# Two of the four set-aside scores of an attention turn, computed and copied in halves of 256 queries

## The chip, the cores and the metric

The kernel runs on one core of a Trainium2 chip. The metric is the device time of one execution in microseconds (us). A run of the kernel before took 1273.32 us (the median of three, from 1272.75 to 1273.88).

## The reference, cut to what matters

```python
def reference(A_x, A_wqkv, A_wo, B_x, B_w1, B_b1, B_w2, B_b2):
    xn = layernorm(A_x)                                   # (1, 2048, 512)
    qkv = (xn @ A_wqkv).reshape(B, S, 3, 32, 16)          # 32 heads of 16
    scores = einsum("bhqd,bhkd->bhqk", q, k) * 16 ** -0.5
    s = (softmax(scores) @ v) @ A_wo                      # (1, 2048, 512)
    h = relu(xn @ B_w1 + B_b1) ** 2                       # 512 -> 1792
    g = silu(h @ B_w2 + B_b2)                             # 1792 -> 512
    return A_x + s * g
```

All of it is in float32. Attention has 32 heads and 2048 x 2048 scores for each.

## The kernel before, in words

**Stages.** A first stage (about the first 150 us) normalizes x, projects queries, keys and values, and stores queries and keys, each as a high and a low part, so that one contraction over 64 rows gives the score of one head in nearly full precision. Then comes the long stage that the change is in: 128 turns, from about 150 us to about 1250 us. A tail multiplies the last attention output by wo.

**Steps and turns.** A step (`steps`) is one group of four heads (`qd`), one chunk of 512 queries (`qc`) and one block of 128 keys (`kb`): 8 x 4 x 16 = 512 steps. Each step has four heads: pair `p` in 0, 1 and half `hp` in 0, 1. `score(i, p, hp, dst)` is one matmul of 64 rows by 128 columns by 512 queries; `hp` 0 uses the upper 64 rows of the TensorE array and `hp` 1 the lower 64, so two matmuls of different `hp` that follow each other run beside each other. A turn handles four steps. For three of them, `scores(i, p)` computes both heads of a pair into one of two two-bank PSUM tiles (tag S), and `exps(i, p, src)` takes the exponential of both on ScalarE, from PSUM into an SBUF tile `ptile[i, p]`.

**The set-aside step.** The fourth step of a turn, `i + 3`, does not use the S tiles. Its four heads go one at a time through a single PSUM bank, the tile `single` of 128 x 512 float32: `aside(i, p, hp)` issues the score matmul into `single` and a VectorE copy from `single` into half of `ptile[i, p]`. Later ScalarE takes the exponential of `ptile[i, p]` in place. There is one such bank, so each set-aside matmul has to come after the copy of the one before.

**What fills the array.** The feed-forward layer (and later the projection by wo) is spread over the turns as blocks of matmuls of 64 rows by 128 columns by 512. `lin(0)` issues the next one for the upper 64 rows, `lin(1)` for the lower, `lin(0, 1)` one of each; they accumulate in the two banks of the tile `spare`. Next to a set-aside score, which uses only half of the rows, stands a single `lin` of the other half: `lin(0)` with a score of `hp` 1, `lin(1)` with one of `hp` 0.

**Order of a turn.** It is written out by hand. TensorE, VectorE and ScalarE each run their instructions in this order; the framework adds the semaphores. In 120 of the 128 turns the second branch below is taken. (The other branch, which the change leaves alone, belongs to the 8 turns whose block both begins and ends in the same turn.)

```python
        else:
            lin(0)
            aside(i + 3, 0, 1)
            exps(i + 2, 0, scores(i + 2, 0))
            lin(0, 1)
            lin(0, 1)
            exps(i + 2, 1, scores(i + 2, 1))
            aside(i + 3, 1, 0)
            lin(1)
            exps(i + 3, 0, ptile[i + 3, 0])
```

Ahead of it stand the two `scores` of step `i + 1`, with the first set-aside score beside a `lin(1)` between them, and four `lin(0, 1)`; behind it four `lin(0, 1)` and the two `scores` of step `i + 4`, with the fourth set-aside score beside a `lin(0)` ahead of the second of them.

At the end of a turn, `values(i)` to `values(i + 3)` multiply the exponentials of the four steps by the values, into the bank `acc` (line 538). What VectorE has to do besides (evicting `spare`, splitting weights, row sums) is issued at the turns' ends.

**Lines.** In the profile line 282 is the score matmul (its output is named S or `lin`; `lin` is the tag of the tile `single`), line 305 the copy of a set-aside score, line 286 the exponential, line 330 a matmul of the filling work, line 538 the values.

Of the kernel before, what the change touches and what calls it, by code (L numbers as in the profile page):

```python
# [46 lines left out]
@with_exitstack  # L47
def mha_ffn_kernel(ctx: ExitStack, tc: tile.TileContext, x, wqkv, wo, bx, w1, b1, w2, b2, out):
    nc = tc.nc
    x, out = x[0], out[0]  # L50
    ctx.enter_context(tc.manual_schedule())
    keep = ctx.enter_context(tc.tile_pool(name="keep", bufs=1))
    dram = ctx.enter_context(tc.tile_pool(name="dram", bufs=1, space=DRAM))

    ident = keep.tile([128, 128], FT, name="ident")
    make_identity(nc, ident)
    vt = keep.tile([128, NK, VW], FT, name="vt")
    nvalid = keep.tile([1, 1], I32, name="nvalid")
    stat = keep.tile([128, 80], FT, name="stat")

    kdram = [[dram.tile([128, 2, 1024], FT, name=f"kd{g}_{h}") for h in range(2)] for g in range(4)]
    qdram = [[dram.tile([128, 2, 512], FT, name=f"qd{g}_{c}") for c in range(NC)] for g in range(4)]
    xdram = [dram.tile([128, 2, 4, 512], FT, name=f"xd{c}") for c in range(3)]

    udram = [[dram.tile([2, 2, 16, 4, 512], FT, name=f"ud{g}_{c}") for c in range(NC)] for g in range(4)]
    zdram = [[dram.tile([4, 512], FT, name=f"zd{q}_{c}") for c in range(NC)] for q in range(NQ)]
    gdram = dram.tile([S, D], FT, name="gd")

    with tc.tile_pool(name="sb", bufs=1) as sb, tc.tile_pool(name="ps", bufs=1, space=PSUM) as ps:
        fast_path(tc, sb, ps, locals())  # L70
    general_path(tc, dram, nvalid, ident, vt, kdram, qdram, gdram, x, wo, out)


def fast_path(tc, sb, ps, env):
# [6 lines left out]
    mm = nc.tensor.matmul  # L81
    dve, act, pool, sp = nc.vector, nc.scalar, nc.gpsimd, nc.sync
# [3 lines left out]
    def t(shape, dt, tag):  # L86

        cnt[0] += 1
        p = ps if tag in ("S", "lin", "acc") else sb
        if tag in BUFS:  # L90
            turn[tag] = turn.get(tag, -1) + 1
            n = turn[tag] % BUFS[tag]
            tag = f"{tag}{places[n] if tag == 'S' else n}"
        return p.tile(shape, dt, tag=tag, name=f"{tag}_{cnt[0]}")
# [180 lines left out]
    steps = [(qd, qc, kb) for qd in range(NQ) for qc in range(NC) for kb in range(NK)]  # L275
    ptile = {}

    def score(i, p, hp, dst):
        qd, qc, kb = steps[i]
        k, q = ka[qd, kb // 8], qa[qd, qc]  # L280
        r = slice(64 * hp, 64 * hp + 64)
        mm(dst, k[r, p, 128 * (kb % 8):128 * (kb % 8) + 128], q[r, p], start=True, stop=True)  # L282

    def exps(i, p, src):
        if src is not None:
            act.activation(ptile[i, p], src, AF.Exp, scale=SCALE)  # L286

    def place(i, p):
        ptile[i, p] = t([128, 2, 512], FT, f"P{2 * ((i - 1) % 4) + p}")

    def scores(i, p):

        if i < len(steps):
            sc = t([128, 2, 512], FT, "S")
            place(i, p)
            for hp in range(2):
                score(i, p, hp, sc[:, hp])
            return sc

    def aside(i, p, hp):  # L300

        if hp == 0:
            place(i, p)
        score(i, p, hp, single)
        dve.tensor_copy(ptile[i, p][:, hp], single)  # L305

    gated, complete, gates = {}, set(), set()

# [30 lines left out]
    def lin(*halves):  # L339
        if pair[0]:  # L340
            for half in halves:
                j = half ^ swapped[0]
                pair[0][j].issue(half, lin_banks[j])

    def swap():
        if pair[0]:
            while any([pair[0][half ^ swapped[0]].issue(half, lin_banks[half ^ swapped[0]]) for half in range(2)]):
                pass
            swapped[0] ^= 1
            if not swapped[0]:  # L350
                pair[0][0].evict()
                pair[0] = None
# [21 lines left out]
    def split_piece(eng=None):  # L374
        if at_piece[1] == len(pieces):
            return
        j, layer, m = pieces[at_piece[1]]
        at_piece[1] += 1
        raw, q = raws.pop(0), PAIRS[m][1]
        wf[layer, m] = [t([128, 4, 256] if layer == 1 else [128, 2, 512], FR, f"wf{layer}{p}{q}") for p in "hl"]  # L380
        split(*wf[layer, m], raw, eng or dve, pool)
        load_piece()
# [149 lines left out]
    def values(i):  # L532
        qd, qc, kb = steps[i]
        if kb == 0:
            acc[0] = t([128, 512], FT, "acc")
        for j in (1, 2, 3, 0) if i % 2 else (0, 1, 2, 3):
            o = (4 * qd + j) * 17
            mm(acc[0][32 * j:32 * j + 32], vt[:, kb, o:o + 32], ptile[i, j // 2][:, j % 2],  # L538
               start=kb == 0, stop=kb == NK - 1)

    def finish(i):

        qd, qc, kb = steps[i]
        if kb < NK - 1:
            return
        if i == len(steps) - 1:
            return
        ou = t([128, 512], FT, "ou")
        cast(act if turn_ends_first[0] else dve, ou, acc[0])
        sp.dma_start(zdram[qd][qc], ou[16::32])  # L550
        for j in range(4):
            sp.dma_start(udram[qd // 2][qc][0, qd % 2, :, j], ou[32 * j:32 * j + 16])
        n = i // 4
        events.setdefault(2 * n + 2, []).insert(0, (load_sums, (qd, qc)))
        at(n + 2, rowsums, qd, qc)
# [174 lines left out]
    def happen(time):  # L730
        for fn, a in events.pop(int(2 * time), ()):
            fn(*a)


    n = turn["S"]
# [4 lines left out]
    single = t([128, 512], FT, "lin")  # L740
    xs[0] = xT[3]

    def rest(i, dst):

        group(dst, lambda p: onorm[2, 3][p][:, cut[i]], lambda p: wos[0][p][:, 3])

    def end_rest(i, src):

        o = t([128, 512], FT, f"wf2{'hl'[i // 2]}{i % 2}")
        dve.scalar_tensor_tensor(o, src, 0.5, gsb[2, i // 2][:, i % 2], op0=OP.mult, op1=OP.mult)  # L750
        pool.dma_start(out[1024 + 128 * i:1152 + 128 * i], o, accum_op=OP.add)

    turn_ends_first = [False]
    for n in range(TURNS):
        i = 4 * n
        happen(n)
        make, end, split_now = fill[n]
        if make:
            pair[0] = make()
        exps(i + 1, 0, scores(i + 1, 0))  # L760
        aside(i + 3, 0, 0)
        lin(1)
        exps(i + 1, 1, scores(i + 1, 1))
        for _ in range(5 if make and end else 4):
            lin(0, 1)
        if make and end:
# [3 lines that stand above are left out]
            swap()  # L770
# [5 lines that stand above are left out]
            last = [scores(i + 4, 0)]  # L776
            for _ in range(4):
                lin(0, 1)
        else:
            lin(0)  # L780
            aside(i + 3, 0, 1)
            exps(i + 2, 0, scores(i + 2, 0))
            lin(0, 1)
            lin(0, 1)
            exps(i + 2, 1, scores(i + 2, 1))
            aside(i + 3, 1, 0)
            lin(1)
            exps(i + 3, 0, ptile[i + 3, 0])
            lin(0, 1)
            lin(0, 1)  # L790
            last = [scores(i + 4, 0)]
# [3 lines that stand above are left out]
        aside(i + 3, 1, 1)  # L795
        exps(i + 3, 1, ptile[i + 3, 1])
        last.append(scores(i + 4, 1))
        for p in range(2):
            exps(i + 4, p, last[p])
        if n == TURNS - 1:  # L800
            two = t([128, 2, 512], FT, "S")
            rest(0, two[:, 0])
        turn_ends_first[0] = n < LAST and end and fill[n][0] is None and fill[n - 1][2] and n % per in (7, 15, 23)
        swap()
        if n == LAST - 1:
            gsb.update({(2, i): y[2, i] for i in range(2)})
        if n == TURNS - 1:
            end_rest(0, two[:, 0])
        happen(n + 0.5)
        if split_now:  # L810
            split_piece()
        for j in range(4):
            values(i + j)
        finish(i + 3)
# [5 lines left out]
    zc, r = t([128, 16], FT, "zc"), t([128, 16], FT, "rc")  # L820
# [15 lines left out]
    for i in range(4):  # L836
        for j in range(4):
            mm(small[32 * j:32 * j + 32, 0, cut[i]], r[:, 4 * i + j:4 * i + j + 1].broadcast_to([128, 32]), ident,
               start=True, stop=True)
# [138 lines left out]
```

## Time and profile before

| | before |
|---|---|
| median of 3 runs | 1273.32 us |
| profiled execution, its time | 1272.96 us |
| span in the profile | 1271.1 us |
| TensorE matmuls (PE) | 1257.3 us busy, 9925 instructions |
| TensorE weight loads (PEld) | 721.4 us busy |
| ScalarE (ACT) | 1034.2 us busy |
| VectorE (DVE) | 678.5 us busy, 1065 instructions |
| granted TensorE clock | 0.998 |

The span runs from the first to the last instruction that the profiler recorded; the profiled execution's time is 1.86 us longer. PE is the matmul side of TensorE and PEld its weight loads, which have rows of their own. A matmul's recorded duration includes its way through the array, so two that follow each other overlap in the records: how often one can start is read from the start times, not from the durations.

### The profile page before, as it was taken

The page shows a single profiled execution, that of the slowest core. Times are in us where ns is not written, and L with a number is a line of the kernel's source. Part 1 is how long each engine was busy: PE and PEld are TensorE (multiplying, and loading weights), DVE is VectorE, ACT ScalarE, POOL GpSimd, SP SyncE. Part 2 cuts the span into 40 slices and gives each one's busy share as a digit, 9 for nine tenths or more (in the row PEclk, how much of TensorE's full clock was granted, in tenths as well). Part 3 has the DMA queues.
Part 4 walks back from the last instruction along what each step waited for, and adds up shares of the span by engine and source line. Part 5 has one row for each costly group of instructions (what it writes and reads, how often), then busy time and mean ns, then how long its engine had stood idle before and what let it go on. Part 6 is the DMA issues. An engine that isn't in the chain of part 4 may idle for free.

```text
span 1271.1 us, 24788 instructions
## 1 busy us (share of the span) xinstructions
PE 1257.3 (99%) x9925; PEld 721.4 (57%) x9925; DVE 678.5 (53%) x1065; ACT 1034.2 (81%) x1123; POOL 257.8 (20%) x149
## 2 busy tenths in 40 slices
PE   9999999999999999999999999999999999999996
PEld 7888755555555455555555555555555555545553
DVE  5542255455555654545465455555554545566655
ACT  4222588889899898898988889899889988998883
POOL 5000122122211221312022221220331212322111
PEclk9999999999999999999999999999999999999999
DMA  7565513131233132121423222333222132463445
GB/s 266 206 232 197 217 43 102 58 93 59 77 125 109 59 105 64 45 87 48 152 73 109 60 76 60 93 125 108 58 60 87 47 89 59 142 216 125 143 129 118
DMA packets 84940, 137.32 MB, mean 108 GB/s; under 512 B 26058, under 2 KB 40408, under 8 KB 83284
## 3 DMA queue, kind: packets, MB, share of 16 engines
q1 hardware_dynamic: 81668, 126.25, 30.9%
q0 software_dynamic: 2720, 8.65, 2.3%
q8 instruction: 79, 1.29, 0.4%
q10 hardware_dynamic: 432, 0.79, 0.2%
q14 instruction: 41, 0.34, 0.1%
HBM read 94.24 MB, written 41.41 MB: 107 GB/s over the span
## 4 chain that ended last, share of the span: by engine, by line
PE 96%; DVE 2%; ACT 1%; POOL 0%; DMA 0%; issue 0%; ACTq 0%; DVEq 0%
PE acc L538 36%; PE spare L330 26%; PE S L282 16%; PE S L111 9%; PE lin L282 7%; DVE P L305 1%; PE S L204 1%; POOL hl L104 0%; DMA P<-in_A_x_dram 0%; PE acc L111 0%; DVE st L166 0%; DVE P L858 0%; ACT P L286 0%; DVE P L864 0%; ACT wf2h L98 0%
## 5 line engine op out<-in xcount | busy, mean ns | idle before, releaser
L286 ACT ACTIVATE P<-S 128x1024 f32<-128x1024 f32 x768 | 732.4, 1020 | 67.9 <-PE S L282 64.5
L305 DVE COPY P<-lin 128x512 f32<-128x512 f32 x512 | 354.1, 692 | 467.6 <-PE lin L282 342.7
L538 PE MATMUL acc<-P,vt 128*32 128x512 f32 x4096 | 466.0, 595 | 0.0
L282 PE MATMUL S<-QA,KA 64*128 64x512 f32 x1536 | 332.8, 422 | 0.1
L286 ACT ACTIVATE P<-P 128x1024 f32<-128x1024 f32 x256 | 271.4, 1060 | 43.7 <-DVE P L305 43.6
L538 PEld LDWEIGHTS acc<-P,vt 128*32 128x32 f32 x4096 | 120.2, 110 | 272.9 <-issue 272.9
L282 PEld LDWEIGHTS S<-QA,KA 64*128 64x128 f32 x1536 | 145.3, 184 | 159.9 <-ACT P L286 142.6
L282 PE MATMUL lin<-QA,KA 64*128 64x512 f32 x512 | 213.2, 416 | 1.0 <-DVE P L305 0.3
L104 POOL TENSOR_TENSOR wf1l<-wr,wf1h 128x1024 fp32r<-128x1024 f32 x28 | 66.8, 2384 | 404.5 <-DVE wf1h L100 135.3
L330 PE MATMUL spare<-xl,wf1h 64*128 64x512 f32 x504 | 122.3, 400 | 0.0
L104 POOL TENSOR_TENSOR hl<-T,hh 128x1024 fp32r<-128x1024 f32 x28 | 67.6, 2415 | 242.2 <-PE S L282 131.3
L104 POOL TENSOR_TENSOR wf2l<-wr,wf2h 128x1024 fp32r<-128x1024 f32 x28 | 66.7, 2383 | 207.4 <-PE acc L538 139.1
L330 PE MATMUL spare<-wf2l,hh 64*128 64x512 f32 x448 | 107.1, 399 | 0.0
L282 PEld LDWEIGHTS lin<-QA,KA 64*128 64x128 f32 x512 | 94.2, 184 | 22.3 <-DVE P L305 13.6
L330 PE MATMUL spare<-xh,wf1l 64*128 64x512 f32 x504 | 96.3, 392 | 0.0
L330 PE MATMUL spare<-xh,wf1h 64*128 64x512 f32 x504 | 95.5, 390 | 0.0
L330 PE MATMUL spare<-wf2h,hh 64*128 64x512 f32 x448 | 87.7, 392 | 0.0
L330 PE MATMUL spare<-wf2h,hl 64*128 64x512 f32 x448 | 84.6, 391 | 0.0
L330 PEld LDWEIGHTS spare<-xl,wf1h 64*128 64x128 f32 x504 | 67.0, 185 | 8.2
L330 PEld LDWEIGHTS spare<-xh,wf1h 64*128 64x128 f32 x504 | 60.0, 185 | 9.8
L330 PEld LDWEIGHTS spare<-xh,wf1l 64*128 64x128 f32 x504 | 59.8, 185 | 8.4
L98 ACT CAST P<-S 128x512 fp32r<-128x512 f32 x30 | 17.6, 587 | 57.7 <-PE S L111 55.9
(201 smaller groups left out, 995.6 us busy)
## 6 DMA issues: line engine op xcount, KB each, us to landing
wr<-in_B_w_dram SPq DMA_DIRECT2D x56, 512.0 KB
KA<-kd SPq DMA_DIRECT2D x64, 256.0 KB
QA<-qd SPq DMA_DIRECT2D x128, 128.0 KB
kd<-P SPq DMA_DIRECT2D x15, 512.0 KB
qd<-P SPq DMA_DIRECT2D x15, 512.0 KB
u<-ud SPq DMA_DIRECT2D x15, 512.0 KB
P<-in_A_x_dram SPq DMA_DIRECT2D x8, 512.0 KB
xd<-KA SPq DMA_DIRECT2D x4, 1024.0 KB
```

The lines of the kernel that those rows point to most:

```text
L98: act.copy(dst, src)
L104: leng.tensor_tensor(lo, src, hi.bitcast(FT), op=OP.subtract)
L111: mm(dst, lhs(a, k), rhs(b, k), start=n == 0, stop=n == len(todo) - 1)
L204: nc.tensor.transpose(pt[:, k, 128 * j:128 * j + 128], xnorm[c, i][:, j, 128 * k:128 * k + 128], ident)
L282: mm(dst, k[r, p, 128 * (kb % 8):128 * (kb % 8) + 128], q[r, p], start=True, stop=True)
L286: act.activation(ptile[i, p], src, AF.Exp, scale=SCALE)
L305: dve.tensor_copy(ptile[i, p][:, hp], single)
L330: mm(bank, self.lhs(a, k)[r], self.rhs(b, k)[r], start=n == 0 and self.at[other] == 0, stop=n == len(self.todo[half]) - 1 and self.at[othe ...
L538: mm(acc[0][32 * j:32 * j + 32], vt[:, kb, o:o + 32], ptile[i, j // 2][:, j % 2], start=kb == 0, stop=kb == NK - 1)
```

## The change

A new helper `aside_half` does what `aside` does for 256 of the 512 queries: a score matmul of 256 columns into one half of the bank `single`, and a copy of that half. In the second branch of a turn the second set-aside score becomes two such halves one right behind the other, and the third one becomes two halves with the single `lin(1)` between them. The first and the fourth stay whole. In each of the 120 turns two matmuls of 512 columns and two copies of 512 are replaced by four of 256.

```diff
-    def score(i, p, hp, dst):
+    def score(i, p, hp, dst, cols=slice(0, 512)):
         qd, qc, kb = steps[i]
         k, q = ka[qd, kb // 8], qa[qd, qc]
         r = slice(64 * hp, 64 * hp + 64)
-        mm(dst, k[r, p, 128 * (kb % 8):128 * (kb % 8) + 128], q[r, p], start=True, stop=True)
+        mm(dst, k[r, p, 128 * (kb % 8):128 * (kb % 8) + 128], q[r, p, cols], start=True, stop=True)
...
+    def aside_half(i, p, hp, n):
+
+        if hp == n == 0:
+            place(i, p)
+        s = slice(256 * n, 256 * n + 256)
+        score(i, p, hp, single[:, s], s)
+        dve.tensor_copy(ptile[i, p][:, hp, s], single[:, s])
...
             lin(0)
-            aside(i + 3, 0, 1)
+            for m in range(2):
+                aside_half(i + 3, 0, 1, m)
             exps(i + 2, 0, scores(i + 2, 0))
             lin(0, 1)
             lin(0, 1)
             exps(i + 2, 1, scores(i + 2, 1))
-            aside(i + 3, 1, 0)
+            aside_half(i + 3, 1, 0, 0)
             lin(1)
+            aside_half(i + 3, 1, 0, 1)
             exps(i + 3, 0, ptile[i + 3, 0])
```

## The prediction

> **What bounds the kernel now.** I read the page's busy shares first, then the waits, then one turn in the timeline, engine by engine. From the page:
>
> ```profile
> span 1271.1 us, 24788 instructions
> ## 1 busy us (share of the span) xinstructions
> PE 1257.3 (99%) x9925; PEld 721.4 (57%) x9925; DVE 678.5 (53%) x1065; ACT 1034.2 (81%) x1123; POOL 257.8 (20%) x149
> ```
>
> TensorE has work in flight nearly all the time; VectorE, which has to make the added copies, is idle for almost half of it. How long a turn takes follows from the set-aside matmuls, grouped by the tile they write:
>
> ```profile
> L282 PE MATMUL lin<-QA,KA x512: 383/393/503, 150.1 to 1248.3; 64*128 64x512 f32 x171
> ```
>
> That is 512 = 128 turns of four, the first at 150.1 us and the last at 1248.3. The last is the fourth of its turn, which starts 4.10 us after the first one (610.66 against 606.56 in the next fence), so 127 turns take 1094.1 us, 8.61 us each. The timeline of one turn, TensorE's matmuls:
>
> ```profile
> 606.22 0.50 PE L282 MATMUL S<-QA,KA 64*128 64x512 f32 x2
> 606.56 0.39 PE L282 MATMUL lin<-QA,KA 64*128 64x512 f32 x1
> 606.56 0.39 PE L330 MATMUL spare<-wf2h,hh 64*128 64x512 f32 x1
> 606.79 0.39 PE L282 MATMUL S<-QA,KA 64*128 64x512 f32 x2
> 607.02 1.09 PE L330 MATMUL spare<-wf2h,hh 64*128 64x512 f32 x7
> ...
> 607.96 0.39 PE L282 MATMUL lin<-QA,KA 64*128 64x512 f32 x1
> 607.96 0.39 PE L330 MATMUL spare<-wf2l,hh 64*128 64x512 f32 x1
> 608.18 0.40 PE L282 MATMUL S<-QA,KA 64*128 64x512 f32 x2
> 608.41 0.63 PE L330 MATMUL spare<-wf2l,hh 64*128 64x512 f32 x4
> 608.87 0.45 PE L282 MATMUL S<-QA,KA 64*128 64x512 f32 x2
> 609.16 0.49 PE L282 MATMUL lin<-QA,KA 64*128 64x512 f32 x1
> 609.16 0.72 PE L330 MATMUL spare<-wf2l,hh 64*128 64x512 f32 x2
> 609.50 0.65 PE L330 MATMUL spare<-wf2h,hl 64*128 64x512 f32 x3
> 609.96 0.41 PE L282 MATMUL S<-QA,KA 64*128 64x512 f32 x2
> ...
> 610.66 0.39 PE L282 MATMUL lin<-QA,KA 64*128 64x512 f32 x1
> ...
> 611.22 3.64 PE L538 MATMUL acc<-P,vt 128*32 128x512 f32 x32
> 614.79 0.50 PE L282 MATMUL S<-QA,KA 64*128 64x512 f32 x2
> ```
>
> This turn runs from 606.22 to 614.79, 8.57 us. Two matmuls of 64 rows start together and the next two 0.23 us later (606.56, 606.79, 607.02): call that a slot. The turn has 20 slots, 4.6 us, and the values from 611.22 to 614.79, 3.57 us: 8.17 of 8.57. So there is about 0.4 us of stalls in a turn; the matmul stream sets its length, and whatever stops TensorE for longer is paid for. Some 0.17 of the 0.4 lies between 608.87 and 609.50, where two slots take 0.63 us instead of 0.46. The other engines in the same turn, VectorE, ScalarE and the weight loads:
>
> ```profile
> 608.41 0.69 DVE L305 COPY P<-lin 128x512 f32<-128x512 f32 x1 [0.66 <-PE lin L282]
> 609.76 0.69 DVE L305 COPY P<-lin 128x512 f32<-128x512 f32 x1 [0.66 <-ACT P L286]
> 606.82 3.80 ACT L286 ACTIVATE P<-S 128x1024 f32<-128x1024 f32 x4 [0.59 <-PE S L282]
> 611.92 1.06 ACT L286 ACTIVATE P<-P 128x1024 f32<-128x1024 f32 x1 [0.36 <-DVE P L305]
> 609.16 0.18 PEld L282 LDWEIGHTS lin<-QA,KA 64*128 64x128 f32 x1 [0.16 <-DVE P L305]
> ```
>
> The second set-aside matmul starts at 607.96, its copy at 608.41 (0.45 later) and ends at 609.10; the weight load of the third starts at 609.16, 0.06 after that, and says that it waited for a copy. ScalarE waits in two places of the turn, 0.59 and 0.36 us, so it has room.
>
> **The change, part by part.** It moves no DMA, and nothing on GpSimd's or SyncE's queue. In 120 turns it makes of two set-aside matmuls four, and of two copies four: 240 instructions more on TensorE and on VectorE each. The rows for their sizes:
>
> ```profile
> L305 DVE COPY P<-lin 128x512 f32<-128x512 f32 x512 | 354.1, 692 | 467.6 <-PE lin L282 342.7 <-ACT P L286 74.8 <-PE spare L330 48.6
> L104 DVE TENSOR_TENSOR P<-S,P 128x512 fp32r<-128x512 f32 x30 | 20.8, 692 | 58.7 <-ACT P L98 58.7
> L849 DVE TENSOR_TENSOR P<-S,P 128x256 f32<-128x256 f32 x2 | 0.8, 420 | 1.0 <-PE lin L846 1.0
> L282 PEld LDWEIGHTS lin<-QA,KA 64*128 64x128 f32 x512 | 94.2, 184 | 22.3 <-DVE P L305 13.6
> ```
>
> *Copies.* No row has a copy of 256 columns. A two-operand instruction that reads PSUM takes 692 ns for 512 columns, as the copy does, and 420 ns for 256; I take 0.42 us. VectorE gets 240 x (2 x 0.42 - 0.69) = 36 us more. It is idle for 467.6 us ahead of these copies, so that alone costs nothing.
>
> *Does the second half wait for the first half's copy?* This decides the sum, and no row shows it: nowhere in this trace does a matmul write one part of a bank while VectorE reads another part of it. The nearest rows are the reuses of this same bank, where the next matmul starts 0.06 us after the copy's end. The two halves are different columns, but one bank and one tile. At one end the second half waits for nothing and the pair costs what the whole did; at the other it waits as a whole score does. I take the wait, because every reuse of the bank that the rows show is such a handover.
>
> The Trainium skill, "PSUM — Partial Sum Buffer", section "PSUM bank collisions raise a hardware error", says that two engines may not touch one bank of a 32-partition quadrant at the same time, disjoint columns included, and that one has to guard by bank, not by address. By it the wait is certain; no run shows it yet.
>
> *Second score, the two halves in a row.* Half a slot is 0.115 us. From the first half's start to its copy: 0.45 - 0.115 = 0.335. Copy: 0.42. Handover: 0.06. The second half's weight load has then to be made in the open: the third set-aside score, whose load waited, takes 0.34 from 609.16 to the next pair at 609.50 instead of 0.23, so 0.11. Then its columns, 0.115. In all 1.04 us until its rows of the array are free, where the whole took 0.23: 0.81 us more on those 64 rows. The other 64 may go on when the second half starts to stream, 0.115 earlier: 0.69 more. Queued behind the waiting load on TensorE are the scores of step i + 2, two `lin` pairs and the third set-aside score; ScalarE waits for those scores. Nothing covers the wait: the `lin(0)` beside it takes one slot and began with the first half.
>
> *Third score, with `lin(1)` between.* `lin(1)` uses the other 64 rows and runs beside the first half, as it ran beside the whole, so it covers nothing more. From the third matmul's start to its copy (609.16 to 609.76) are 0.60, less the open weight load of 0.11 and half a slot: 0.375. Then 0.42 + 0.06 + 0.11 + 0.115: 1.08 in all, 0.85 above a slot. Behind it wait four `lin` pairs, a score pair, the fourth set-aside score and the values.
>
> *What goes.* The copy of the second score's second half ends 0.815 + 0.11 + 0.335 + 0.42 = 1.68 us after the first half's start. The third score comes five slots after the first half, 1.15, plus the 0.69 to 0.81 that were lost: 1.84 or later. So it no longer waits, and the 0.17 us of stall between 608.87 and 609.50 go.
>
> *Sum.* The second score's late rows are 64 to 127, the third's are 0 to 63. If each half of the rows runs on by itself, the long path takes 0.69 + 0.85; if they stay in step, 0.81 + 0.85. Less 0.17: 1.37 to 1.49 us a turn. One more bound: a weight load lasts 184 ns, more than half a slot, so the load after each second half may show by up to 0.07, at both places 0.14. That makes 1.37 to 1.63; I take 1.45, near the lower end, since the rows show loads beside running matmuls. 120 x 1.45 = 174 us. Against the profiled execution's own time, 1272.96 us (span 1271.1 and 1.86 around it; 0.36 under the median of the runs), that is **1447 us**.
>
> On the open load: the row at 609.16 shows that a load which waits for a copy is not made ahead, and that its pair takes 0.11 longer. The Trainium skill, "TensorE: Matmul & The Clock Gate", section "Step-by-step: what each phase is for", says that TensorE pulls weight loads ahead of running matmuls when the row groups do not conflict or the load goes to the background buffer. If the halves' loads were pulled ahead by that rule, both 0.11 would go: 1.23 a turn, an estimated 1421 us; the trace speaks against it where the load itself carries the wait.
>
> **The rivals.** *No wait between the halves, and faster.* If only columns count, the third score's first half needs only the first half's copy, done 0.335 + 0.42 + 0.06 = 0.82 us after the second score's start, and the 0.17 us of stall between 608.87 and 609.50 go with nothing added: 120 x 0.17 = 20 us less, 1253 us. It decides where a matmul may write columns of a bank while others are read. For it speaks that the third score's wait is in the rows (0.16 on its load); against it, that the matmul after a copy of this bank has in every row come behind it.
>
> *No wait, and slower.* As before, but a load of 184 ns for 115 ns of columns shows at both places: 120 x 2 x 0.07 = 17 us, 1290 us if the old stall stays.
>
> *The wait falls into idle time that is there anyway.* The waits view has
>
> ```profile
> PEld S L282 <- ACT P L286: 142.6, 277, 0.8
> PEld lin L282 <- DVE P L305: 13.6, 63, 0.6
> ```
>
> and the timeline of the weight loads
>
> ```profile
> 614.79 0.19 PEld L282 LDWEIGHTS S<-QA,KA 64*128 64x128 f32 x2 [0.84 <-ACT P L286]
> ```
>
> If TensorE stood still for the 142.6 us of the first row, a longer stop elsewhere would use them up: 174 - 143 = 31 us, 1304 us. Against it: in the quoted turn the longest such wait ends at 614.79, right behind the values matmuls, so it is the weight side that idles there while matmuls run.
>
> *The change does nothing.* The copies are hidden and the columns are the same in number; if neither wait nor load shows, 1273 us. The third score's wait speaks against it in both directions.
>
> **How the numbers follow.** About 0.2% (2.5 us) is what a measurement of this kernel can tell from no change. Chances: the wait at both places 0.85; swallowed by idle time 0.04; no wait and slower 0.04; no change 0.02; no wait and faster 0.05. So faster 0.05, same 0.02, slower 0.93. The range lies within the first case. Its low end has no open loads at all and the rows out of step: 1.37 - 0.22 = 1.15 us a turn, 1411 us. Its high end: 1.63, and at each place another 0.11 for a load that is opened behind the wait: 1.85, 1495 us. I take 1410 to 1495.
>
> **What would show it.** Right: in the changed profile 752 set-aside matmuls and 752 copies, 480 of each of 256 columns; such a copy near 420 ns; a second half's matmul in the second score about 0.8 us behind the first half's; `lin` weight loads waiting for line 305 about 240 times in place of 63; turns near 10.0 us; ScalarE and VectorE with about the same work and lower shares; the third score's first half without a wait. Wrong: second halves that start within 0.25 us of the first ones (no wait), turns that stay under 8.8 us, or ScalarE as the one that ends the waits of line 282 at 10 us a turn.

## The result and the profile after

The changed kernel takes 1455.22 us (median of four runs, 1454.34 to 1455.74) against 1273.49 us for the kernel before: a ratio of 1.1426, 95% interval 1.1412 to 1.1441. Forecast were 1447 us, from 1410 to 1495. The spans are 1453.0 and 1271.1 us, so each of the 120 changed turns grew by 181.9 / 120 = 1.516 us on average. In the changed kernel line 313 is the copy of a half, line 338 the filling work and line 546 the values.

The page after, its busy shares, the granted clock, and two of its groups:

```profile
span 1453.0 us, 25508 instructions
...
PE 1326.3 (91%) x10165; PEld 770.5 (53%) x10165; DVE 716.2 (49%) x1305; ACT 1044.5 (72%) x1123; POOL 257.3 (18%) x149
...
PEclk9999999999999999999999999999999999999998
...
L305 DVE COPY P<-lin 128x512 f32<-128x512 f32 x272 | 188.0, 691 | 348.4 <-PE lin L282 220.0
...
L313 DVE COPY P<-lin 128x256 f32<-128x256 f32 x480 | 203.9, 425 | 265.0 <-PE lin L282 167.9
```

TensorE, VectorE and ScalarE all have lower shares: none of them became the bound. VectorE has 37.7 us more work, 36 were expected, and it is still idle for half of the span. The clock row shows that TensorE was not slowed (0.997). The waits view of the kernel after (engine, tile and line that waited, for whom, us in total, times, longest):

```profile
PEld lin L282 <- DVE P L313: 207.1, 244, 1.2
...
ACT P L286 <- PE S L282: 161.6, 226, 1.1
...
PE lin L282 <- DVE P L313: 112.7, 240, 0.7
...
PEld S L282 <- ACT P L286: 112.5, 143, 0.8
```

Weight loads (PEld) of set-aside scores waited for a copy 63 times before; now they wait for a half copy 244 times, four above the 240 second halves, and 240 times the matmul side itself is empty. ScalarE waits for scores 226 times, 161.6 us in all (109 times and 64.5 us before), since they come late; TensorE's waits for ScalarE went from 142.6 to 112.5 us. One turn in the timeline, first TensorE's matmuls, then VectorE's copies and the loads of set-aside scores:

```profile
703.21 0.28 PE L282 MATMUL lin<-QA,KA 64*128 64x256 f32 x1
704.14 0.39 PE L282 MATMUL lin<-QA,KA 64*128 64x256 f32 x1 [0.55 <-DVE P L313]
704.15 0.61 PE L282 MATMUL S<-QA,KA 64*128 64x512 f32 x2
704.49 0.73 PE L338 MATMUL spare<-wf2l,hh 64*128 64x512 f32 x4
704.95 0.51 PE L282 MATMUL S<-QA,KA 64*128 64x512 f32 x2
705.18 0.28 PE L282 MATMUL lin<-QA,KA 64*128 64x256 f32 x1
705.30 0.39 PE L338 MATMUL spare<-wf2l,hh 64*128 64x512 f32 x1
706.07 0.39 PE L282 MATMUL lin<-QA,KA 64*128 64x256 f32 x1 [0.38 <-DVE P L313]
706.08 0.50 PE L338 MATMUL spare<-wf2h,hl 64*128 64x512 f32 x1
706.30 0.39 PE L338 MATMUL spare<-wf2l,hh 64*128 64x512 f32 x1
...
703.66 0.42 DVE L313 COPY P<-lin 128x256 f32<-128x256 f32 x1 [0.66 <-PE spare L338]
704.57 0.42 DVE L313 COPY P<-lin 128x256 f32<-128x256 f32 x1 [0.48 <-PE lin L282]
705.59 0.42 DVE L313 COPY P<-lin 128x256 f32<-128x256 f32 x1 [0.60 <-PE lin L282]
706.50 0.42 DVE L313 COPY P<-lin 128x256 f32<-128x256 f32 x1 [0.48 <-PE lin L282]
...
704.14 0.18 PEld L282 LDWEIGHTS lin<-QA,KA 64*128 64x128 f32 x1 [0.90 <-DVE P L313]
...
705.04 0.18 PEld L282 LDWEIGHTS lin<-QA,KA 64*128 64x128 f32 x1
...
706.07 0.18 PEld L282 LDWEIGHTS lin<-QA,KA 64*128 64x128 f32 x1 [0.82 <-DVE P L313]
```

The chain of a hand-over is read straight off: first half at 703.21, its copy at 703.66, done at 704.08, the second half's load at 704.14. Between 703.21 and 704.14 no further matmul starts. The third score does the same from 705.18 to 706.07, and the `lin(1)` between its halves starts at 705.30, beside the first half, and hides none of it. The third score's own first load, at 705.04, waits for nothing.

### The profile page after: what moved, and what is told of

The parts are those of the page before. It is cut to its first block, busy times and chain, and to the rows that moved or that the text cites. A ratio compares the mean times of both kernels' runs of the same rounds, so it can differ in the third digit from the quotient of the medians.

```text
span 1453.0 us, 25508 instructions
## 1 busy us (share of the span) xinstructions
PE 1326.3 (91%) x10165; PEld 770.5 (53%) x10165; DVE 716.2 (49%) x1305; ACT 1044.5 (72%) x1123; POOL 257.3 (18%) x149
## 4 chain that ended last, share of the span: by engine, by line
PE 88%; DVE 9%; issue 2%; ACT 0%; POOL 0%; DMA 0%; DVEq 0%; ACTq 0%
PE acc L546 31%; PE spare L338 23%; PE S L282 14%; PE lin L282 10%; PE S L111 8%; DVE P L313 7%; PE S L204 0%; DVE P L305 0%; POOL hl L104 0%; DMA P<-in_A_x_dram 0%; PE acc L111 0%; DVE st L166 0%; DVEq L313 0%; DVE P L868 0%; DVE P L874 0%
## 5 line engine op out<-in xcount | busy, mean ns | idle before, releaser
L286 ACT ACTIVATE P<-S 128x1024 f32<-128x1024 f32 x768 | 742.4, 1019 | 164.4 <-PE S L282 161.6
L282 PE MATMUL S<-QA,KA 64*128 64x512 f32 x1536 | 385.7, 419 | 0.1
L282 PE MATMUL lin<-QA,KA 64*128 64x256 f32 (+1 forms) x752 | 266.9, 355 | 113.2 <-DVE P L313 112.7
L305 DVE COPY P<-lin 128x512 f32<-128x512 f32 x272 | 188.0, 691 | 348.4 <-PE lin L282 220.0
L313 DVE COPY P<-lin 128x256 f32<-128x256 f32 x480 | 203.9, 425 | 265.0 <-PE lin L282 167.9
L282 PEld LDWEIGHTS S<-QA,KA 64*128 64x128 f32 x1536 | 196.1, 184 | 120.0 <-ACT P L286 112.5
L282 PEld LDWEIGHTS lin<-QA,KA 64*128 64x128 f32 x752 | 138.1, 184 | 214.7 <-DVE P L313 207.1
L338 PE MATMUL spare<-xh,wf1l 64*128 64x512 f32 x504 | 115.6, 403 | 0.0
L338 PE MATMUL spare<-wf2h,hl 64*128 64x512 f32 x448 | 98.2, 401 | 0.0
L338 PEld LDWEIGHTS spare<-xl,wf1h 64*128 64x128 f32 x504 | 79.5, 185 | 3.5
L338 PEld LDWEIGHTS spare<-wf2l,hh 64*128 64x128 f32 x448 | 69.9, 185 | 3.9
```

What stands on the lines that cost most here:

```text
L313: dve.tensor_copy(ptile[i, p][:, hp, s], single[:, s])
L338: mm(bank, self.lhs(a, k)[r], self.rhs(b, k)[r], start=n == 0 and self.at[other] == 0, stop=n == len(self.todo[half]) - 1 and self.at[othe ...
```

## The experiments

**Halved matmuls and halved copies, each alone.** The cost could lie in the added matmuls, in the added copies, or only in the two together.

```diff
 def aside_half(i, p, hp, n):
...
-        dve.tensor_copy(ptile[i, p][:, hp, s], single[:, s])
+        if n == 1:
+            dve.tensor_copy(ptile[i, p][:, hp], single)
```

> The second and third set-aside matmuls are in halves of 256 columns as in the changed kernel, but one copy of 512 columns follows the second half, so nothing is handed over between the halves. Theory (the hand-over between the halves is the cost): near the kernel before, 1273 us, plus at most 0.07 us a place for a weight load of 184 ns behind 115 ns of columns, 120 x 2 x 0.07 = 17 us: 1273 to 1290 us. Rival (240 more matmuls with their weight loads cost the time themselves): near the changed kernel, 1455 us.

Measured: 1272.02 us, ratio 0.9988 (0.9978 to 0.9997). Where nothing is handed over between them, the 240 more matmuls and weight loads cost nothing.

```diff
 def aside_half(i, p, hp, n):
...
-        score(i, p, hp, single[:, s], s)
+        if n == 0:
+            score(i, p, hp, single)
```

> The matmuls are whole as before, and the copy of the second and third set-aside score is in halves. Theory (the hand-over is the cost): two copies of 0.425 us end 0.16 us later than one of 0.69, and the third set-aside matmul, which already waits for the copy before it, waits that much longer: 120 x 0.16 = 19 us, 1292 us. Rival (the 240 more copies on VectorE cost the time): near the changed kernel, 1455 us.

Measured: 1282.60 us, ratio 1.0069 (1.0052 to 1.0086): 9 us, half of what was expected. Its copies in the timeline, two to a row:

```profile
612.26 0.76 DVE L314 COPY P<-lin 128x256 f32<-128x256 f32 x2 [0.67 <-PE lin L282]
...
613.07 0.18 PEld L282 LDWEIGHTS lin<-QA,KA 64*128 64x128 f32 x1 [0.22 <-DVE P L314]
```

Two half copies in a row take 0.76 us, not 2 x 0.42, so the third score is held up by 0.07 us more than by one copy of 0.69: 120 x 0.07 = 8 us. The place is the one expected, the size was too high. So the halved matmuls alone cost nothing and the halved copies alone 9 of the 182 us; the rest comes when a matmul has to wait between two copies.

**One place at a time.** In the first the third score is whole again, in the second the second score.

```diff
-            aside_half(i + 3, 1, 0, 0)
+            aside(i + 3, 1, 0)
             lin(1)
-            aside_half(i + 3, 1, 0, 1)
```

> Only the second set-aside score is in halves. Theory (hand-over, and the two row halves of the array run on by themselves): the lower rows are late by 0.93 + 0.11 + 0.115 - 0.23 = 0.93 us, the stall of 0.17 us at the third score goes: 0.76 us a turn, 91 us, 1364 us. Rival (each place costs half of the whole change): 1364 us too; this run alone does not tell them apart, together with the next it does.

```diff
-            for m in range(2):
-                aside_half(i + 3, 0, 1, m)
+            aside(i + 3, 0, 1)
```

> Only the third set-aside score is in halves. Theory (hand-over, rows run on by themselves): 0.89 + 0.11 + 0.115 - 0.23 = 0.885 us a turn on the upper rows, and the old stall of 0.17 us ahead of the third score stays, since the second score is whole: 106 us, 1379 us; the two single changes add up to 197 us, 15 more than both together. Rival (each place costs half of the whole): 91 us, 1364 us. Rival (the lin(1) between the halves covers part of the wait, as it stands there for 0.23 us): 78 us, 1351 us.

Measured: 1371.16 us (ratio 1.0769, 1.0752 to 1.0787) and 1372.04 us (1.0771, 1.0753 to 1.0789), against 1273.86 us for the kernel before beside them: 97.3 and 98.2 us. Neither hit its number: the second score is 6 us above its expectation, the third 8 us below its own and 7 above the rival's 91. Together they are 195.5 us, 13.8 more than the 181.7 us of the change. That is 0.115 us a turn, half a slot, as expected where each half of the array's rows runs on by itself; since both parts missed, the sum is a sign of that and no proof. The timeline after is plainer: the third score starts at 705.18 on the upper rows and `lin(1)` at 705.30 on the lower, where before both started at 609.16. The third score's price of 0.82 us a turn rules out that `lin(1)` covers part of it (0.65). Why that place came out 8 us cheaper than expected is not traced to the end. For the second score alone the trace shows where more was lost. Its loads of the second score pair of step `i + 2` and of the two pairs of step `i + 4`:

```profile
612.00 0.30 PEld L282 LDWEIGHTS S<-QA,KA 64*128 64x128 f32 x2
...
613.21 0.19 PEld L282 LDWEIGHTS S<-QA,KA 64*128 64x128 f32 x2 [0.21 <-ACT P L286]
...
614.12 0.19 PEld L282 LDWEIGHTS S<-QA,KA 64*128 64x128 f32 x2 [0.15 <-ACT P L286]
```

The stall at the second pair of step `i + 2` is gone, as expected, but both pairs of step `i + 4` now wait for ScalarE, which was fed late (it waited 162.6 us for scores, 64.5 before). So in that run part of the old stall came back there.

**A first half ahead of `lin(0)`.** In the changed kernel the half matmul's copy started 0.45 us after it, as after a whole one.

```diff
-            lin(0)
-            for m in range(2):
-                aside_half(i + 3, 0, 1, m)
+            aside_half(i + 3, 0, 1, 0)
+            lin(0)
+            aside_half(i + 3, 0, 1, 1)
```

> As the changed kernel, but the first half of the second set-aside score is issued ahead of the lin(0) that runs beside it instead of behind it. In the changed kernel its copy starts 0.454 us after the half matmul, as after a whole one. Theory (a matmul reports its end no earlier than the one issued ahead of it, here a whole lin(0)): with the half first the copy starts 0.335 us after it, 0.118 us a turn are saved, 14 us: 1441 us. Rival (the copy starts 0.45 us after any matmul, however short): no change, 1455 us.

Measured: 1438.37 us, ratio 1.1297 (1.1277 to 1.1318), 17 us below the changed kernel. In its timeline:

```profile
706.50 0.27 PE L282 MATMUL lin<-QA,KA 64*128 64x256 f32 x1
706.51 0.40 PE L338 MATMUL spare<-xl,wf1h 64*128 64x512 f32 x1
...
706.81 0.42 DVE L313 COPY P<-lin 128x256 f32<-128x256 f32 x1 [0.51 <-PE lin L282]
```

The same two matmuls, beside each other as before, but the copy starts 0.31 us after the half instead of 0.45. The semaphore records of these two turns say the same without VectorE: in the changed kernel the half's end is told 0.43 us after its start, 0.03 behind that of `lin(0)`, and here 0.29 after its start. So the end of the short matmul had been told no earlier than that of the longer one issued ahead of it on the other 64 rows. 14 us were expected, 17 came.

**The hand-over taken away.** All eight banks are in use, so a second one has to be bought: the base leaves out the filling work of the lower 64 rows, so that its feed-forward results are not the reference's, lets the upper rows use one bank, and gives the first stage two S tiles instead of three. Then the halved kernel is run on that base, once through one bank, once with a bank for each half; the diff shows how the last differs from the one before it.

```diff
 def aside_half(i, p, hp, n):
...
-        score(i, p, hp, single[:, s], s)
-        dve.tensor_copy(ptile[i, p][:, hp, s], single[:, s])
+        bank = second_bank if n else single
+        score(i, p, hp, bank[:, s], s)
+        dve.tensor_copy(ptile[i, p][:, hp, s], bank[:, s])
```

> The kernel before with one PSUM bank made free: the filling work of the lower 64 rows is left out and that of the upper rows goes to one bank (so the feed-forward and projection results are not the reference's), and the first stage has two S tiles instead of three. The base for the next two runs. Slots keep their length, since the upper rows still fill them: near 1273 us, up to 15 us more for the first stage.

> The changed kernel, with the filling work of the lower rows left out and one bank free as in f0_room; both halves still go through the one bank. Theory and rivals: as the change itself, some 180 us above f0_room (170 to 195).

> As f1_room_halves, but the second half of a score goes to the free bank, a tile of its own. Same matmuls, same copies, no hand-over between the halves. Theory (the wait for the first half's copy is the cost): the time falls back to that of f0_room, between 20 us under it (the stall of 0.17 us at the third score goes, since its first half needs only the copy of a first half) and 17 us above it (weight loads behind short matmuls). Rival (half matmuls and half copies cost the time wherever they go): near f1_room_halves. Rival (copies that take turns on VectorE become late, so that ScalarE waits): 40 us or more above f0_room.

Measured: 1278.82 us for the base, 1578.65 us through one bank, 1274.27 us with two banks. With two banks the same matmuls and the same copies take 4.6 us less than whole scores do in the base. From that run's timeline:

```profile
612.72 0.38 PE L282 MATMUL lin<-QA,KA 64*128 64x256 f32 x1
...
612.95 0.28 PE L282 MATMUL second<-QA,KA 64*128 64x256 f32 x1
...
614.08 0.27 PE L282 MATMUL lin<-QA,KA 64*128 64x256 f32 x1
614.19 0.32 PE L282 MATMUL second<-QA,KA 64*128 64x256 f32 x1
```

The second halves start 0.23 and 0.11 us after the first ones instead of 0.93 and 0.89. The second bank is also a tile of its own, and the wait is a semaphore that the framework puts in: whether it goes by the bank or by the tile, no run here tells. The run through one bank missed its number: 300 us above its base, not 170 to 195. Its windows of 10 us (busy time and instructions of PE, PEld, DVE, ACT and POOL, then granted clock, DMA share and GB/s):

```profile
300.00:310.00 10.00, 8.86 (x63) 4.72 (x62) 6.31 (x10) 7.64 (x9) 2.37 (x1) 1.00 0.34 106
...
320.00:330.00 10.00, 9.45 (x52) 3.86 (x52) 5.04 (x7) 5.58 (x7) 2.37 (x1) 0.74 0.03 6
330.00:340.00 10.00, 9.41 (x51) 3.96 (x49) 3.89 (x9) 5.88 (x6) 2.36 (x1) 0.66 0.22 62
```

and the first half of the second score in two turns of its timeline:

```profile
363.66 0.38 PE L282 MATMUL lin<-QA,KA 64*128 64x256 f32 x1
...
373.73 0.38 PE L282 MATMUL lin<-QA,KA 64*128 64x256 f32 x1
```

Its clock fell to a mean of 0.911; the base and the two-bank run had 0.998 and 0.996. A turn at full clock lasts 10.07 us there (363.66 to 373.73), as in the changed kernel. In the base the same place stands at 613.89 and 622.44, 8.55 apart. So the hand-overs make 120 x 1.52 = 182 us of the 300, as was expected, and the rest went with the slower clock, which was not.

**A version that might beat both.** If distance to the copy before is what a set-aside score costs, whole scores further apart should take away the stall of 0.17 us. In the first run a `lin(0, 1)` is moved ahead of the third score, in the second ahead of the score pair in front of it.

```diff
             exps(i + 2, 1, scores(i + 2, 1))
+            lin(0, 1)
             aside(i + 3, 1, 0)
             lin(1)
             exps(i + 3, 0, ptile[i + 3, 0])
             lin(0, 1)
-            lin(0, 1)
```

> The kernel before, with one lin(0, 1) moved from behind the third set-aside score to ahead of it; no halves. Theory (what a set-aside score costs is the distance to the copy before it): the second copy ends 1.15 us after its matmul starts, the third score would start 1.43 us after it instead of 1.20, so its wait and the open weight load of 0.11 us go: 0.11 to 0.17 us a turn, 13 to 20 us, 1253 to 1260 us. Rival (the fourth score then stands too near to the third copy, 1.17 us behind its matmul against 1.15 to 1.29 needed, and the stall only moves): 1273 us.

```diff
+            lin(0, 1)
             exps(i + 2, 1, scores(i + 2, 1))
             aside(i + 3, 1, 0)
             lin(1)
             exps(i + 3, 0, ptile[i + 3, 0])
             lin(0, 1)
-            lin(0, 1)
```

> The kernel before, with one lin(0, 1) moved ahead of the second score pair of step i + 2, so that this pair and the third set-aside score both come a slot later; no halves. Theory (distance): the third score's wait and open load go, and the pair's short wait for ScalarE too: 0.17 us a turn, 20 us, 1253 us. Rival (ScalarE gets that pair 0.23 us later and has no work in between, and every exponential behind it is late): 1273 us or more, as far as ScalarE's own waits of 0.36 us a turn do not take it up.

Measured: 1284.37 us (ratio 1.0082, 1.0068 to 1.0096) and 1276.20 us (1.0019, 1.0010 to 1.0028); the first is slower than the kernel before by 10 us, the second by 2. Neither saved the 13 to 20 us of the theory; the first is worse than its rival too, and the second came out as its rival said. The first run's timeline:

```profile
612.73 0.19 PEld L282 LDWEIGHTS S<-QA,KA 64*128 64x128 f32 x2 [0.21 <-ACT P L286]
...
613.66 0.19 PEld L282 LDWEIGHTS S<-QA,KA 64*128 64x128 f32 x2 [0.18 <-ACT P L286]
...
613.80 0.69 DVE L305 COPY P<-lin 128x512 f32<-128x512 f32 x1 [0.79 <-PE lin L282]
...
614.54 0.50 PE L282 MATMUL lin<-QA,KA 64*128 64x512 f32 x1
```

The third score waits no longer, but the fourth now starts 0.05 us after the third's copy ends (613.80 + 0.69 = 614.49; before it was 0.21), with an open load, and a second score pair waits for ScalarE. In the second run's timeline

```profile
610.57 0.19 PEld L282 LDWEIGHTS S<-QA,KA 64*128 64x128 f32 x2 [0.21 <-ACT P L286]
...
610.64 0.69 DVE L305 COPY P<-lin 128x512 f32<-128x512 f32 x1 [0.73 <-PE lin L282]
...
611.39 0.49 PE L282 MATMUL lin<-QA,KA 64*128 64x512 f32 x1
```

it is the first pair of step `i + 4` that waits for ScalarE, and the fourth score again stands right behind the third's copy (610.64 + 0.69 = 611.33). My theory left out that its neighbours stand nearly as tight. No run here beats the kernel before by more than the 0.1% of the halved matmuls with one copy.

## Why the prediction was right

The likeliest case was the one that came, and its mechanism was shown from three sides: in the trace after, by halving matmuls and copies each alone, and by the second bank. Step by step:

- **The wait.** Chosen as the case, and there at both places in every turn. What the Trainium skill says of banks in "PSUM — Partial Sum Buffer", section "PSUM bank collisions raise a hardware error", pointed the same way. No run here lets a matmul write a bank that is being read, so the rule itself was not tried, and what the runs show is the framework's wait and its price.
- **The copy and the hand-over.** 0.42 and 0.06 us were taken; the trace has 0.425 and 0.06.
- **From the first half's start to its copy.** This is the term that was mis-sized. I took 0.335 us for the second score, the whole matmul's time less half a slot; it is 0.45, because the half stands behind a whole `lin(0)` and its end is told no earlier. The run with the half first shows 0.31. At the third score I took 0.375, and it is 0.41; no run tried that place.
- **The open weight load behind a wait.** 0.11 us was taken from the third score of before. After the change the second half and the upper score beside it start at 704.14 and the next pair at 704.49, 0.34 later instead of 0.23, so 0.11 again: the waiting load was not made ahead, and the estimate of 1421 us by the rule of the Trainium skill ("TensorE: Matmul & The Clock Gate", section "Step-by-step: what each phase is for") was low.
- **Loads behind short matmuls.** Up to 0.14 us a turn was allowed for them. They cost nothing: the halved matmuls with one copy are no slower than before.
- **Rows that run on by themselves.** I let them, for the lower bound of the sum. They do: in the timeline after, the upper rows are 0.12 us ahead at the third score, and the two single places add up to half a slot a turn more than both together.
- **The old stall.** The third score waits no more, and from 704.95 to 705.18 is one plain slot. That the 0.17 us go was right here, where TensorE is late for everything, but not as a rule: with the second score alone in halves, or with the order changed, later scores of the turn waited in its place.

The lower sum, 1.37 us, and the two corrections, 0.115 and 0.035, make 1.52 us a turn; 1.516 were measured. I had taken 1.45, which allowed 0.08 for loads that cost nothing or rows that stay in step, and nothing for the late end: two misses of opposite sign, and 8 us in the end. That the number came so near is partly luck; the lower sum alone would have given 1437 us.

The rivals fell on the profile: the second halves start 0.93 and 0.89 us behind the first, far from 0.25; and the waits for ScalarE lost only 30 of their 142.6 us, so they did not swallow the hand-overs.

## What to carry to other kernels

Work through one buffer costs a full round trip each time it changes hands, and splitting the work doubles the round trips and shortens each by less than half: 0.93 us for half a score here, against 1.20 for a whole one. Split only where each part has a buffer of its own, or, which no run here tried, where the program puts as much other work between the parts as the trip takes. Before moving a step away from a wait, look at the distances of its neighbours: in a tight order the stall goes to the next one.

## What the runs showed of the hardware

- A short matmul on one half of the array's rows told its end only with the longer matmul issued ahead of it on the other half: 0.45 us to the copy, and 0.31 us when it was issued first. The Trainium skill has the rule, "TensorE: Matmul & The Clock Gate", Part 3, section "The mechanism": matmuls start and end in program order. The trace agrees for the end told here. It does not for the start. Both halves of the rows work through the same list, and at 705.30 `lin(1)` had taken the last `wf2l` of the lower rows; so behind the third score the `wf2l` at 706.30 is the upper rows' `lin(0)`, and the lower rows' `lin(1)`, which follows it in the program, started ahead of it at 706.08.
- Two copies of 256 columns behind each other took 0.76 us, though each is recorded with 0.42: the second starts 0.34 us after the first, while the first is still recorded as running.
- The granted clock fell to 0.911 in the one run where the lower rows had no filling work and TensorE also stopped twice a turn. Either alone left it at 0.996 to 0.998, and the longest wait of a set-aside matmul for a copy was 0.9 us. Which of the two the clock reacts to, and from what point, stays open.
